# Second network's weight conversion moved off GpSimd, and the fourth and fifth chunk cut at 512 and 384 tokens

## Chip, cores and metric

The kernel runs on one core of a Trainium2 chip. The metric is the device time of one execution in microseconds (us). Engines are named as the profile names them: PE is TensorE, DVE is VectorE, ACT is ScalarE, POOL is GpSimd, SP is the engine whose queue issues the DMAs.

## What is computed

Attention over 4 batches, 8 heads, 576 positions and 64 channels gives 2304 tokens of 512 channels. They go through a gated feed-forward of width 1536 and then through a second feed-forward that takes the largest of three products, of width 768:

```python
scores = q @ k.T / 8                      # 4 heads: the last 32 positions; 4 heads: every 32nd position
x = softmax(where(mask, scores, -1e9)) @ v
g = x @ w_gate
x = (g * sigmoid(g) * (x @ w_val)) @ w_out
h = maximum(maximum(x @ w1, x @ w2), x @ w3)
out = h @ w2_out
```

The weights arrive as 64-bit numbers and are turned into 32-bit ones on the chip.

## The kernel before

**Tiles.** The 2304 tokens are 72 rows of 32 tokens (`ORDER`, l.43), cut into five chunks by `ROWS` (l.40): 512, 448, 448, 448 and 448 tokens. Each chunk goes through the first feed-forward in 12 blocks f of 128 hidden channels. A block is 36 matmuls: `emit_gate` (l.716) 12 into `ps_g`, `emit_val` (l.723) 12 into `ps_v`, `emit_out` (l.767) 12 into the four sums `ps_y`. Each product of 128 x 128 weights is three matmuls (l.701 to 703), since operands are split into a high and a low part. Between them lie a Silu on ACT (l.720), a multiply on DVE (l.727), a copy to the high part on ACT (l.733) and the low part on POOL (l.737). `ps_g` and `ps_v` share two PSUM buffers, so a product can start only when the one two before has been read.

**Order.** The first chunk (f = 0 to 11, with attention for the first two chunks and the conversion of the first network's weights) runs in an order written by hand, `FIRST`. The next four chunks are laid out by the loop at l.1080: block by block, with attention for the chunk after next to come spread over `attention_steps` (l.653), and with steps that convert the second network's weights. A scheduler then decides the order within each engine. `PACE` (l.35) says how many of those conversion steps each of the first ten blocks of a chunk brings; there are 60, five for each of 12 pairs of weight tiles.

**A conversion step.** For a pair (`pair_steps`, l.259): load two tiles of 512 KB; for each tile `size` and `rounding` on ACT (l.202, 205), `sign` (l.207), a clamp on DVE (l.219), `shift` and `rounded` on DVE (l.221, 229); then `combine` (l.263) makes the four sums of the seven-product scheme that the second network uses; then `part` (l.276) splits the results into high parts (ACT, l.281) and low parts (l.282) and stores them to DRAM in eight DMAs. `sign` has two forms: on ACT, for keys that stand in `ON_SCALAR` among the first network's tiles, or on POOL, for all others. With the first form `shift` has one input, with the second two.

**Strided attention.** Of four heads, the rows that PE doesn't take are done by `Unit` (l.567) on DVE: up to six rows at once, multiplies and reductions (l.600, 603, 622, 625), then transposes on PE (l.632).

**The seam.** After block f = 9 of the last chunk (`SEAM`) the attention buffers are freed, `load_y` (l.827) loads the first tokens of the second network, and `Factors.combine` and `Factors.split` (l.805, 812) make its operands during f = 10 and f = 11, in an order that is fixed by hand. The second network (l.858) then runs 1512 matmuls of 384 columns. All loads and stores are issued by SP, in order; the reloads of the first network's weights for each block (l.1018) stand in the same queue as the loads and stores of the conversion.

Of the kernel before, what the change touches and what calls it, by code (L numbers as in the profile page):

```python
# [7 lines left out]
F32 = mybir.dt.float32  # L8
# [5 lines left out]
ALU = mybir.AluOpType  # L14
AX = mybir.AxisListType

B, H, S, D = 4, 8, 576, 64
# [3 lines left out]
NI = S // STRIDE  # L21

LR = 2
# [8 lines left out]

PASSES = [1, 2, 0]

PACE = [0, 0.7, 1.4, 1.4, 3.1]

PACED = 10
NK = DM // 128

ROWS = [0, 16, 30, 44, 58, 72]  # L40


ORDER = [*range(16), *range(18, 72), 16, 17]
# [50 lines left out]
def tile_attention_swiglu_maxout(  # L94
# [13 lines left out]
    nc = tc.nc  # L108
# [31 lines left out]
    def f32(ap):  # L140
        return ap.bitcast(F32)
# [49 lines left out]
    made = {}  # L191

    def signed(key):
        return key in order and order.index(key) in ON_SCALAR

    def words(key):
        if key not in made:
# [61 lines left out]
    def pair_steps(i, g):  # L259
        keys = [(i, 2 * g), (i, 2 * g + 1)]  # L260
        made = {}

        def combine():
            w1t, w2t = (cvt.pop(k) for k in keys)
            s12 = wpool.tile([128, 512], F32, name="s12", tag="w")
            s4 = wpool.tile([128, 512], F32, name="s4", tag="w")[:, :256]
            a11, a12, a21, a22 = w1t[:, :256], w1t[:, 256:], w2t[:, :256], w2t[:, 256:]
            if i == 3:
                a12, a21 = a21, a12
            nc.vector.tensor_tensor(s12[:, :256], a21, a22, ALU.add)  # L270
            nc.vector.tensor_tensor(s12[:, 256:], s12[:, :256], a11, ALU.subtract)
            nc.gpsimd.tensor_tensor(a21, a11, a21, ALU.subtract)
            nc.vector.tensor_tensor(s4, a12, s12[:, 256:], ALU.subtract)
            made["full"] = [w1t, w2t, s12, s4]

        def part():
            dst = wsdr[i, g].rearrange("p (c s n) -> p c s n", c=7, s=2)
            for n, full in enumerate(made.pop("full")):
                w = full.shape[1]
                hi = wpool.tile([128, 512], F32R, name="whi", tag="w")[:, :w]  # L280
                nc.scalar.activation(hi, full, AF.Copy)
                (nc.gpsimd if n % 2 else nc.vector).tensor_tensor(full, full, f32(hi), ALU.subtract)
                for p, src in enumerate((f32(hi), full)):
                    nc.sync.dma_start(
                        dst[:, 2 * n:2 * n + w // 256, p], src.rearrange("p (c n) -> p c n", n=256)
                    )

        return [
            lambda: [load(k, w2[k[1], :, k[0], :]) for k in keys],
            lambda: convert(keys[0]),  # L290
            lambda: convert(keys[1]),
            combine,
            part,
        ]

# [228 lines left out]
    def local_block(g, home=None):  # L524


        def dst(src, us):
            for c, i0, i1, o in pieces(LR * g[0], LR * (g[-1] + 1)):
                t, w = slice(i0 * STRIDE, i1 * STRIDE), slice(o * STRIDE, (o + i1 - i0) * STRIDE)
                xh, xl = x_tile(c)  # L530
                yield xh[:, 0:2, t], xl[:, 0:2, t], src[:, :, w]

        return Block((locqk, locv), g[0], KB, [mask[0 if n % (NI // LR) == 0 else 1] for n in g], dst, home=home)
# [33 lines left out]
    class Unit:  # L567
# [36 lines left out]

        def softmax(self):
            sc, n, jn = self.sc, self.n, self.jn
            mx = tiny.tile([128, 6], F32, name="smx")[:, :n]
            nc.vector.tensor_reduce(mx, sc, AX.X, ALU.max)
            nc.vector.tensor_tensor(sc, sc, mx[:, :, None].to_broadcast([128, n, jn]), ALU.subtract)
            nc.scalar.activation(sc, sc, AF.Exp, scale=SCALE)  # L610
            sums = tiny.tile([128, 6], F32, name="ssum")[:, :n]
            nc.vector.tensor_reduce(sums, sc, AX.X, ALU.add)
            nc.vector.tensor_scalar(sums, sums, 1.0e-9, None, ALU.add)
            nc.vector.reciprocal(sums, sums)
            nc.vector.tensor_tensor(sc, sc, sums[:, :, None].to_broadcast([128, n, jn]), ALU.mult)
            self.o = st_p[0].tile([128, 6, D], F32, name="sto")

        def pv(self, r, eng):
            i = self.i0 + r
# [25 lines left out]

    def attention_blocks(c):
        rows = ORDER[ROWS[c]:ROWS[c + 1]]
        blocks = [local_block(g) for g in joined([r // LR for r in rows[::LR]])]
        if c == 1:
            blocks += [strided_block((st1qk, st1v), 1, g) for g in pairs(range(STRIDE // ON_PE[1][2]))]  # L650
        return blocks

    def attention_steps(c):

        steps = [[] for _ in range(15)]
        rows = ORDER[ROWS[c]:ROWS[c + 1]]
        eng = nc.vector
        blocks = attention_blocks(c)
        at = [0, 0, 4, 4, 8]
        for n, blk in enumerate(blocks):  # L660
            s0 = at[n]
            wait = 3 if c == 2 and s0 == 0 else 0
            steps[max(0, s0 - 2)].append(blk.load)
            if n % 2 and s0 == at[n - 1]:
                steps[s0].append(lambda a=blocks[n - 1], b=blk: a.scores_with(b))
                steps[s0 + wait].append(lambda a=blocks[n - 1], b=blk: (a.softmax(eng), b.softmax(eng)))
            elif n + 1 == len(blocks) or s0 != at[n + 1]:
                steps[s0].append(lambda blk=blk: (blk.scores(), blk.softmax(eng)))
            steps[s0 + (4 if wait else 1)].append(lambda blk=blk: blk.transpose(nc.scalar))
            if n % 2 and s0 == at[n - 1]:  # L670
                steps[s0 + (5 if wait else 2)].append(lambda a=blocks[n - 1], b=blk: (a.outputs_with(b), a.split(), b.split()))
            elif n + 1 == len(blocks) or s0 != at[n + 1]:
                steps[s0 + 2].append(blk.pv)
        units = []
        on_pe = {n: rows for n, rows, _ in ON_PE}
        left = [r for r in rows if r % NI >= on_pe.get(r // NI, 0)]
        while left:
            i = left[0]
            n = 1
            while n < len(left) and left[n] == i + n and (i + n) % NI % 6:  # L680
                n += 1
            units.append(Unit(i // NI, i % NI, n))
            left = left[n:]
        s0 = 0
        for u in units:
            steps[s0].append(u.load)
            steps[s0].append(u.begin)
            for r in range(u.n):
                steps[s0 + (2 * r // u.n)].append(lambda u=u, r=r: u.qk(r, eng))
            steps[s0 + 2].append(u.softmax)  # L690
            for r in range(u.n):
                steps[s0 + 2 + (2 * r // u.n)].append(lambda u=u, r=r: u.pv(r, eng))
            for r in range(0, u.n, 3):
                steps[s0 + 5 + r // 3].append(lambda u=u, r=r: u.out(r))
            s0 += 4
        return steps


# [555 lines left out]
```

## Time and profile before

| | us |
|---|---|
| median of 3 runs | 785.13 (785.03 to 786.27) |
| the profiled execution | 786.19 |
| its span, first to last instruction | 784.4 |
| PE busy | 767.7 (98%) |
| DVE busy | 613.2 (78%) |
| ACT busy | 400.9 (51%) |
| POOL busy | 230.8 (29%) |

The profile follows one execution. Busy times are sums over instructions of an engine; PE's matmuls overlap, so its busy time says little about how fast they follow each other, and the starts of successive rows in the timeline say it instead. The first chunk ends at about 143 us, the last chunk of the first network runs from 428 to 516 us, the second network from there to the end.

### The profile page before, as it was taken

The page shows a single profiled execution, that of the slowest core. Times are in us where ns is not written, and L with a number is a line of the kernel's source. Part 1 is how long each engine was busy: PE and PEld are TensorE (multiplying, and loading weights), DVE is VectorE, ACT ScalarE, POOL GpSimd, SP SyncE. Part 2 cuts the span into 40 slices and gives each one's busy share as a digit, 9 for nine tenths or more (in the row PEclk, how much of TensorE's full clock was granted, in tenths as well). Part 3 has the DMA queues.
Part 4 walks back from the last instruction along what each step waited for, and adds up shares of the span by engine and source line. Part 5 has one row for each costly group of instructions (what it writes and reads, how often), then busy time and mean ns, then how long its engine had stood idle before and what let it go on. Part 6 is the DMA issues. An engine that isn't in the chain of part 4 may idle for free.

```text
span 784.4 us, 13322 instructions
## 1 busy us (share of the span) xinstructions
PE 767.7 (98%) x4642; PEld 705.2 (90%) x4642; DVE 613.2 (78%) x1206; ACT 400.9 (51%) x925; POOL 230.8 (29%) x226
## 2 busy tenths in 40 slices
PE   5899999999999999999999999999999999999998
PEld 4677788888998998988899999999999999999998
DVE  5999999798959899799796777754689377855683
ACT  6999997644544636545342545432335233433342
POOL 2533332012221432325242556420124111321120
PEclk9999999999999999999999999999999999999999
DMA  9989886987657896847787999997675976878722
GB/s 274 369 277 320 306 351 236 372 252 230 221 188 222 285 293 222 267 168 256 255 286 267 314 378 392 342 377 274 242 276 199 414 270 264 276 280 355 276 101 81
DMA packets 75595, 216.26 MB, mean 276 GB/s; under 512 B 8488, under 2 KB 42024, under 8 KB 70920
## 3 DMA queue, kind: packets, MB, share of 16 engines
q1 hardware_dynamic: 75528, 215.41, 77.8%
q8 instruction: 37, 0.61, 0.3%
q14 instruction: 30, 0.25, 0.1%
HBM read 171.34 MB, written 44.04 MB: 275 GB/s over the span
## 4 chain that ended last, share of the span: by engine, by line
PE 85%; DVE 9%; ACT 3%; issue 1%; DMA 1%; POOL 1%; SPq 0%; DVEq 0%; ACTq 0%
PE ps_a L858 19%; PE ps_c L858 10%; PE ps_v L701 6%; PE ps_y L701 5%; PE ps_y L702 5%; PE ps_v L703 5%; PE ps_y L703 5%; PE ps_v L702 5%; PE ps_g L703 5%; PE ps_g L702 5%; PE ps_g L701 5%; PE ps_b L858 5%; DVE w L231 1%; PE ps_a L504 1%; PE ps_a L462 1%
## 5 line engine op out<-in xcount | busy, mean ns | idle before, releaser
L737 POOL TENSOR_TENSOR hl<-ht,hh 128x448 fp32r<-128x448 f32 x47 | 62.0, 1320 | 215.3 <-ACT hh L733 197.2
L869 ACT ACTIVATE s<-ps_a 128x384 f32<-128x384 f32 x99 | 48.5, 490 | 131.7 <-PE ps_a L858 131.7
L701 PE MATMUL ps_v<-xh,w_v 128*128 128x448 f32 (+1 forms) x240 | 90.8, 379 | 2.1 <-DVE ht L727 1.8
L701 PE MATMUL ps_g<-xh,wh_g 128*128 128x448 f32 (+1 forms) x240 | 89.9, 375 | 1.2 <-DVE ht L760 1.1
L702 PE MATMUL ps_y<-hl,w_o 128*128 128x448 f32 (+1 forms) x240 | 89.6, 373 | 0.0
L702 PE MATMUL ps_g<-xl,wh_g 128*128 128x448 f32 (+1 forms) x240 | 89.5, 373 | 0.0
L703 PE MATMUL ps_g<-xh,wl_g 128*128 128x448 f32 (+1 forms) x240 | 89.3, 372 | 0.0
L703 PE MATMUL ps_v<-xh,w_v 128*128 128x448 f32 (+1 forms) x240 | 89.2, 372 | 0.1
L703 PE MATMUL ps_y<-hh,w_o 128*128 128x448 f32 (+1 forms) x240 | 89.2, 372 | 0.0
L702 PE MATMUL ps_v<-xl,w_v 128*128 128x448 f32 (+1 forms) x240 | 88.9, 370 | 0.0
L733 ACT ACTIVATE hh<-ht 128x448 fp32r<-128x448 f32 (+1 forms) x60 | 35.3, 588 | 94.8 <-DVE ht L727 85.4
L701 PE MATMUL ps_y<-hh,w_o 128*128 128x448 f32 (+1 forms) x240 | 83.6, 376 | 0.0
L808 POOL TENSOR_TENSOR rT<-t,rT 128x384 f32<-128x384 f32 x9 | 12.5, 1392 | 147.1 <-DVE rT L807 147.1
L858 PE MATMUL ps_a<-y0hT,wr 128*128 128x384 f32 x162 | 54.1, 334 | 0.0
L858 PE MATMUL ps_a<-y1hT,wr 128*128 128x384 f32 x162 | 54.1, 334 | 0.0
L701 PEld LDWEIGHTS ps_v<-xh,w_v 128*128 128x128 f32 x240 | 45.1, 188 | 8.1 <-DVE ht L727 2.4
L701 PEld LDWEIGHTS ps_g<-xh,wh_g 128*128 128x128 f32 x240 | 45.1, 188 | 6.8 <-DVE ht L760 1.5
L703 PEld LDWEIGHTS ps_v<-xh,w_v 128*128 128x128 f32 x240 | 45.1, 188 | 5.5 <-DVE w_v L251 0.5
L701 PEld LDWEIGHTS ps_y<-hh,w_o 128*128 128x128 f32 x240 | 45.1, 188 | 5.2
L702 PEld LDWEIGHTS ps_g<-xl,wh_g 128*128 128x128 f32 x240 | 45.1, 188 | 5.1 <-DVE xl L522 0.3
L703 PEld LDWEIGHTS ps_g<-xh,wl_g 128*128 128x128 f32 x240 | 45.1, 188 | 5.1
L703 PEld LDWEIGHTS ps_y<-hh,w_o 128*128 128x128 f32 x240 | 45.1, 188 | 5.0 <-DVE w_o L251 0.3
(257 smaller groups left out, 2070.4 us busy)
## 6 DMA issues: line engine op xcount, KB each, us to landing
wr<-wsdr SPq DMA_DIRECT2D x36, 1792.0 KB, 8.1
raw<-in_w_dram SPq DMA_DIRECT2D x60, 512.0 KB, 6.3
w_v<-wvdr SPq DMA_DIRECT2D x48, 512.0 KB, 4.5
w_o<-wodr SPq DMA_DIRECT2D x48, 512.0 KB, 5.1
wsdr<-whi SPq DMA_DIRECT2D x36, 256.0 KB, 3.4
wvdr<-w_v SPq DMA_DIRECT2D x12, 512.0 KB, 4.6
wodr<-w_o SPq DMA_DIRECT2D x12, 512.0 KB, 6.6
wsdr<-w SPq DMA_DIRECT2D x24, 256.0 KB, 3.9
```

What stands on the lines that cost most here:

```text
L231: nc.vector.tensor_tensor(w, w, q, ALU.add)
L462: nc.tensor.transpose(ps[:sm.shape[2], g * 128:(g + 1) * 128], sm[:, g], ident)
L504: ins = nc.tensor.matmul(ps[j * D:(j + 1) * D, at:at + nq], v, p, start=True, stop=True).ins
L701: nc.tensor.matmul(ps, wh, xh, start=first, stop=False)
L702: nc.tensor.matmul(ps, wh, xl, start=False, stop=False)
L703: nc.tensor.matmul(ps, wl, xh, start=False, stop=last)
L733: return nc.scalar.activation(hs[c, f][0], t, AF.Copy).ins
L737: return eng.tensor_tensor(hl, t, f32(hh), ALU.subtract).ins
L808: nc.gpsimd.tensor_tensor(b12, self.raw["B22"], b12, ALU.subtract)
L858: nc.tensor.matmul(ps, w[:, c, a, ks], b, start=first and n == q == 0, stop=last and n == len(wts) - 1 and q == 2, skip_group_check=True,)
L869: nc.scalar.activation(s, ps, AF.Copy)
```

## The change

It does four things. The fourth and fifth chunk get 16 and 12 rows, 512 and 384 tokens, where they had 14 each. Tiles of the second network take the ACT form of `sign` and the one-input form of `shift`, and their difference in `combine` and all their low parts go to DVE. `PACE` is 0.8, 1.3, 2.0 and 2.0 steps per block in the second to fifth chunk, where it was 0.7, 1.4, 1.4 and 3.1. A `Unit` takes up to eight rows and is cut evenly within a batch, where it was cut at multiples of six; the steps of a chunk's units are spread over 12 divided by their number.

```diff
-PACE = [0, 0.7, 1.4, 1.4, 3.1]
+PACE = [0, 0.8, 1.3, 2.0, 2.0]
+UNIT = 8
-ROWS = [0, 16, 30, 44, 58, 72]
+ROWS = [0, 16, 30, 44, 60, 72]
     def signed(key):
-        return key in order and order.index(key) in ON_SCALAR
+        return key not in order or order.index(key) in ON_SCALAR
...
-            nc.gpsimd.tensor_tensor(a21, a11, a21, ALU.subtract)
+            nc.vector.tensor_tensor(a21, a11, a21, ALU.subtract)
...
-                (nc.gpsimd if n % 2 else nc.vector).tensor_tensor(full, full, f32(hi), ALU.subtract)
+                nc.vector.tensor_tensor(full, full, f32(hi), ALU.subtract)
...
-            while n < len(left) and left[n] == i + n and (i + n) % NI % 6:
+            while n < len(left) and left[n] == i + n and (i + n) % NI:
                 n += 1
-            units.append(Unit(i // NI, i % NI, n))
+            parts = -(-n // UNIT)
+            for p in range(parts):
+                a, b = n * p // parts, n * (p + 1) // parts
+                units.append(Unit(i // NI, i % NI + a, b - a))
             left = left[n:]
-        s0 = 0
-        for u in units:
+        span = 12 // len(units)
+        for u, s0 in zip(units, range(0, 12, span)):
+            half = span // 2
             steps[s0].append(u.load)
             steps[s0].append(u.begin)
             for r in range(u.n):
-                steps[s0 + (2 * r // u.n)].append(lambda u=u, r=r: u.qk(r, eng))
-            steps[s0 + 2].append(u.softmax)
+                steps[s0 + half * r // u.n].append(lambda u=u, r=r: u.qk(r, eng))
+            steps[s0 + half].append(u.softmax)
             for r in range(u.n):
-                steps[s0 + 2 + (2 * r // u.n)].append(lambda u=u, r=r: u.pv(r, eng))
+                steps[s0 + half + half * r // u.n].append(lambda u=u, r=r: u.pv(r, eng))
             for r in range(0, u.n, 3):
-                steps[s0 + 5 + r // 3].append(lambda u=u, r=r: u.out(r))
-            s0 += 4
+                steps[min(14, s0 + span + 1 + r // 3)].append(lambda u=u, r=r: u.out(r))
```

Lines up to about 200 have moved down by two in the changed kernel, those behind `attention_steps` by six, so l.202 is l.204 there, l.720 is l.726 and l.733 is l.739.

The first place is ACT's queue at the start of the fourth chunk, between the Silu of its second block and that of its third (`ht<-ps_g`). Before:

```order
L720 ACTIVATE ht<-ps_g 128x448
L733 ACTIVATE hh<-ht 128x448
L202 ACTIVATE w_4124<-raw 128x512
L205 ACTIVATE q<-raw 128x512
L783 ACTIVATE ysb<-ps_y 128x448 x2
L440 ACT_TABLE_LOAD
L440 ACTIVATE sm,stat<-sm,stat 128x96 x6
L720 ACT_TABLE_LOAD
L720 ACTIVATE ht<-ps_g 128x448
```

With the change:

```order
L726 ACTIVATE ht<-ps_g 128x512
L739 ACTIVATE hh<-ht 128x512
L204 ACTIVATE w_4137<-raw 128x512
L207 ACTIVATE q<-raw 128x512
L204 ACTIVATE w_4145<-raw 128x512
L207 ACTIVATE q<-raw 128x512
L789 ACTIVATE ysb<-ps_y 128x448 x2
L213 ACTIVATE q<-raw,mh 128x512 x2
L442 ACT_TABLE_LOAD
L442 ACTIVATE sm,stat<-sm,stat 128x96 x4
L726 ACT_TABLE_LOAD
L726 ACTIVATE ht<-ps_g 128x512
```

One more tile's size and rounding and the two signs (l.213) stand there now, and four exponentials in place of six.

The second place is DVE's queue at the seam: the multiplies (`ht<-ht,ps_v`), from that of f = 9 to that of f = 10 before, where the last pair's two low parts (l.282) stand ahead of f = 9:

```order
L282 TENSOR_TENSOR w_5596<-w_5596,whi 128x512
L282 TENSOR_TENSOR s_5611<-s_5611,whi 128x512
L727 SCALAR_TENSOR_TENSOR ht<-ht,ps_v 128x448
L807 TENSOR_TENSOR rT_5785<-rT_5762,y0lB_5759 128x384
L178 TENSOR_TENSOR y0lB_5759<-y0lB_5759,y0hB_5792 128x384
L809 TENSOR_TENSOR rT_5788<-y0lB_5765,rT_5785 128x384
L178 TENSOR_TENSOR y0lT_5803<-rT_5785,y0hT_5802 128x384
L178 TENSOR_TENSOR y0lT_5799<-rT_5788,y0hT_5798 128x384
L810 TENSOR_TENSOR rT_5790<-y0lB_5768,rT_5788 128x384
L178 TENSOR_TENSOR y0lB_5768<-y0lB_5768,y0hB_5795 128x384
L727 SCALAR_TENSOR_TENSOR ht<-ht,ps_v 128x448
```

With the change, from the combination that now stands ahead of the multiply of f = 9:

```order
L813 TENSOR_TENSOR rT_5776<-rT_5753,y0lB_5750 128x384
L733 SCALAR_TENSOR_TENSOR ht<-ht,ps_v 128x384
L180 TENSOR_TENSOR y0lB_5750<-y0lB_5750,y0hB_5783 128x384
L815 TENSOR_TENSOR rT_5779<-y0lB_5756,rT_5776 128x384
L180 TENSOR_TENSOR y0lT_5794<-rT_5776,y0hT_5793 128x384
L816 TENSOR_TENSOR rT_5781<-y0lB_5759,rT_5779 128x384
L284 TENSOR_TENSOR w_5587<-w_5587,whi 128x512
L284 TENSOR_TENSOR w_5644<-w_5644,whi 128x512
L284 TENSOR_TENSOR s_5651<-s_5651,whi 128x512
L284 TENSOR_TENSOR s_5652<-s_5652,whi 128x256
L180 TENSOR_TENSOR y0lB_5759<-y0lB_5759,y0hB_5786 128x384
L180 TENSOR_TENSOR y0lT_5790<-rT_5779,y0hT_5789 128x384
```

The four low parts of the last pair (l.284), all on DVE, stand behind the multiply of f = 9 now, and the first combination of y (l.813) ahead of it; the multiply of f = 10 follows the last row shown.

## Rows read from the trace of the kernel before

**Rows 1.** The page, part 1: busy us (share of the span), instructions.

```profile
PE 767.7 (98%) x4642; PEld 705.2 (90%) x4642; DVE 613.2 (78%) x1206; ACT 400.9 (51%) x925; POOL 230.8 (29%) x226
```

**Rows 2.** PE's waits from 143 us on: us in total, times, longest.

```profile
PE ps_v L701 <- DVE ht L727: 1.8, 2, 1.4
PE ps_v L701 <- ACT ht L720: 0.3, 1, 0.3
```

**Rows 3.** Busy times by stretch; columns as in the first line.

```profile
core 0: us, PE busy (x) PEld busy (x) DVE busy (x) ACT busy (x) POOL busy (x), PEclk, DMA share, GB/s
...
238.00:331.00 93.00, 91.56 (x553) 82.93 (x552) 84.69 (x176) 49.97 (x112) 29.23 (x27) 1.00 0.80 263
...
428.20:516.00 87.80, 87.80 (x436) 81.37 (x435) 64.54 (x86) 40.66 (x81) 45.75 (x42) 1.00 1.00 362
```

**Rows 4.** PE's timeline, three stretches: start us, us, instruction.

```profile
47.81 0.50 PE L701 MATMUL ps_v<-xh,w_v 128*128 128x512 f32 x1
48.15 0.39 PE L702 MATMUL ps_v<-xl,w_v 128*128 128x512 f32 x1
...
50.67 0.39 PE L701 MATMUL ps_y<-hh,w_o 128*128 128x512 f32 x1
...
113.19 0.39 PE L701 MATMUL ps_g<-xh,wh_g 128*128 128x512 f32 x1
...
115.91 0.39 PE L701 MATMUL ps_y<-hh,w_o 128*128 128x512 f32 x1
...
450.36 0.36 PE L701 MATMUL ps_g<-xh,wh_g 128*128 128x448 f32 x1
...
457.66 0.36 PE L701 MATMUL ps_g<-xh,wh_g 128*128 128x448 f32 x1
```

**Rows 5.** The chain that ended last, second network: start us, us, what.

```profile
519.78 1.04 PE ps_b L858 x6
```

**Rows 6.** DVE's groups by line and shape: busy us, mean ns, idle before.

```profile
L227 DVE SCALAR_TENSOR_TENSOR w<-w,raw 128x512 int32<-128x512 int32 x39 | 30.5, 791 | 3.3 <-POOL raw L213 2.6 <-POOL w L219 0.5
L219 DVE TENSOR_SCALAR w<-w 128x512 f32<-128x512 f32 x24 | 18.2, 761 | 7.7 <-ACT w L202 7.5
L282 DVE TENSOR_TENSOR w<-w,whi 128x512 f32<-128x512 f32 x12 | 14.6, 1218 | 6.1 <-ACT whi L281 5.5 <-ACT ht L720 0.6
L273 DVE TENSOR_TENSOR s<-w,s 128x256 f32<-128x256 f32 x12 | 10.1, 844 | 0.2
L270 DVE TENSOR_TENSOR s<-w 128x256 f32<-128x256 f32 x9 | 3.7, 413 | 0.1
L600 DVE TENSOR_TENSOR pr<-stk,stq 128x512 f32<-128x512 f32 x2 | 1.4, 688 | 0.0
```

**Rows 7.** DVE's timeline, a clamp in the third chunk.

```profile
305.40 0.43 DVE L219 TENSOR_SCALAR w<-w 128x512 f32<-128x512 f32 x1
```

**Rows 8.** ACT's groups by line and shape: the signs of the first network.

```profile
L211 ACT ACTIVATE q<-raw,mh 128x512 f16<-128x512 int32 x21 | 18.3, 876 | 0.0
```

**Rows 9.** ACT's timeline at the start of the fourth chunk: two Silus.

```profile
345.75 0.55 ACT L720 ACTIVATE ht<-ps_g 128x448 f32<-128x448 f32 x1 [2.00 <-PE ps_g L703]
...
353.66 0.55 ACT L720 ACTIVATE ht<-ps_g 128x448 f32<-128x448 f32 x1
```

**Rows 10.** DVE's timeline at the seam; in brackets the idle time before and its releaser.

```profile
499.81 0.55 DVE L807 TENSOR_TENSOR rT<-rT,y0lB 128x384 f32<-128x384 f32 x1
...
509.38 1.36 DVE L807 TENSOR_TENSOR rT<-rT,y1lB 128x384 f32<-128x384 f32 x1
...
513.89 0.62 DVE L727 SCALAR_TENSOR_TENSOR ht<-ht,ps_v 128x448 f32<-128x448 f32 x1 [0.33 <-PE ps_v L703]
```

**Rows 11.** POOL's groups by line and shape: a combination of the second network's operands.

```profile
L808 POOL TENSOR_TENSOR rT<-y1lB,rT 128x384 f32<-128x384 f32 x3 | 4.2, 1390 | 4.3 <-DVE rT L807 4.3
```

**Rows 12.** DMA issues: count, KB each, median us to landing.

```profile
wr<-wsdr SPq DMA_DIRECT2D x36, 1792.0 KB, 8.1
raw<-in_w_dram SPq DMA_DIRECT2D x60, 512.0 KB, 6.3
...
y0lB<-ydr SPq DMA_DIRECT2D x5, 192.0 KB, 5.6
```

More of the change, by code (lines that the diff above doesn't have):

```diff
@@ L606, in softmax @@
             sc, n, jn = self.sc, self.n, self.jn
-            mx = tiny.tile([128, 6], F32, name="smx")[:, :n]
+            mx = tiny.tile([128, UNIT], F32, name="smx")[:, :n]
             nc.vector.tensor_reduce(mx, sc, AX.X, ALU.max)
@@ L610, in softmax @@
             nc.scalar.activation(sc, sc, AF.Exp, scale=SCALE)
-            sums = tiny.tile([128, 6], F32, name="ssum")[:, :n]
+            sums = tiny.tile([128, UNIT], F32, name="ssum")[:, :n]
             nc.vector.tensor_reduce(sums, sc, AX.X, ALU.add)
@@ L615, in softmax @@
             nc.vector.tensor_tensor(sc, sc, sums[:, :, None].to_broadcast([128, n, jn]), ALU.mult)
-            self.o = st_p[0].tile([128, 6, D], F32, name="sto")
+            self.o = st_p[0].tile([128, UNIT, D], F32, name="sto")
         def pv(self, r, eng):
@@ L647, in attention_blocks @@
         rows = ORDER[ROWS[c]:ROWS[c + 1]]
-        blocks = [local_block(g) for g in joined([r // LR for r in rows[::LR]])]
+        before = {r // LR for r in ORDER[:ROWS[c]]}
+        blocks = [local_block(g) for g in joined([g for g in dict.fromkeys(r // LR for r in rows) if g not in before])]
         if c == 1:
```

## Prediction

> **What bounds the kernel now.** I read three views, from the whole to the place. The page's first part: TensorE (PE) is busy 98% of a 784.4 us span [rows 1]. The list of PE's waits from 143 us on, where the first chunk ends and with it the order written out by hand, has three waits: two for VectorE (DVE), 1.8 us in all, the longest 1.44, and one of 0.3 us for ScalarE (ACT) [rows 2]. The busy times by stage: PE is full and at the full clock, 2.4 GHz, in each; DVE is the next to be full, 84.7 of 93.0 us in the third chunk; in the last chunk it has 64.5 of 87.8, but there the DMA engines' share reads 1.00 at 362 GB/s [rows 3]. So a change pays in two ways only: by what a matmul costs, or by a moment at which PE waits. The first chunk and the second feed-forward (from 516 us) keep their order, so only the four later chunks and the seam into the second network can move.
>
> **1. Widths.** The fourth and the fifth chunk have 432 matmuls each (12 blocks of 36), before and after. At 448 tokens 36 follow each other in 7.30 us, 202.8 ns each; at 512 the pace is 226.7 ns in a quiet stretch (12 in 2.72 us) and 229.1 soon after a break (11 in 2.52 us) [rows 4]; at 384 it is 173.3 (6 in 1.04 us) [rows 5]. Less the columns at 2.4 GHz (213.3, 186.7 and 160.0 ns), 512 and 384 pay 13.4 and 13.3 ns, and 448 pays 16.1. The fourth chunk still has attention's small products inside, so I take 228.5 ns there, and for both chunks of before 203.1, a little over the quiet row: 432 x (228.5 + 173.3 - 2 x 203.1) = **-1.9 us**. Ends: -2.4 by the quiet rows; 0 if the extra 2.8 ns belong to this stage and not to the width, for no row shows 384 in it. Then the breaks: small products split the stream 40 times after the first chunk in the built order, 43 times before, and a break costs 0.11 us (47.81 to 48.15 instead of 0.23) [rows 4]: **-0.3 us**.
>
> **2. Conversions off GpSimd (POOL).** POOL loses 60 operations, five for each of 12 pairs of weight tiles: two signs, two low parts, one difference. DVE gains 36 of them: 12 low parts of 512, 12 of 256, 12 differences of 256. Beside POOL's share of the same work, DVE's own low parts of 512 took 1218 ns and its difference of 256 took 844; such operations apart from it took 688 (512) and 413 (256) [rows 6]. So the new ones cost 12 x 0.69 + 24 x 0.41 = 18.1 us. The old ones should shed 24 x 0.53 (the row of 12 shown has a twin) + 12 x 0.43 = 17.9, and the 24 clamps, at 761 [rows 6] against 430 where one ran alone [rows 7], 24 x 0.33 = 7.9. The shift turns from a form with two inputs, 791 [rows 6], into one with one input, which I price like the clamp: 24 x 0.36 = 8.6. DVE ends 16 us lighter, not heavier.
>
> The rule that speaks against this is in the Trainium skill (Perfetto Trace Analysis, Optimizing Scalar/DVE Operations): offloading from a saturated DVE, even to GpSimd, may make sense. The same section warns that the two share a read port, and rows 6 side with the warning. By the offloading rule alone DVE would be 18.1 us heavier, and this part would be rival (e).
>
> What is it worth? PE was kept for 1.44 us and for 0.36 us by a VectorE multiply that stood behind conversions and attention in DVE's queue [rows 2]. With DVE 16 us lighter I take **-1.8 us**, all of it; the other end is 0 (new waits take their place: attention's rows of the fourth chunk come as two units of eight now and crowd the second and third chunk).
>
> **3. Signs on ACT.** A sign takes 876 ns on ACT [rows 8]; 24 are 21 us on an engine that is half idle, except at one place. At the start of the fourth chunk ACT goes from one Silu to the next, through conversions, evictions, a table load, six exponentials and another table load, from 345.75 to 353.66 [rows 9], and PE is 0.3 us late for that second Silu [rows 2]. In the built order there is one more size and rounding on this way (1.1 us), there are two signs (1.75) and two exponentials less (-0.7): +2.1 us. PE's 36 matmuls meanwhile last 36 x 25.7 ns = 0.9 us longer. **+1.3 us**; ends 0 (if a lighter DVE lets the way begin sooner) and +2.1.
>
> **4. Pace and the seam.** In the last chunk the steps per block fall from 3.1 to 2.0, and the last pair is done one block later, between the multiplies of f = 9 and f = 10. From the multiply of f = 9 to that of f = 11 DVE now has 12 splits and combinations of 384 (0.55 each where alone, as at 499.81 [rows 10]), four low parts (2.4) and two multiplies (1.1): 10.1 us. POOL's five operations in that time, some 1.3 us each (1.39 for a combination [rows 11]), I charge at half their length, 3.3. And a combination now stands ahead of the multiply of f = 9 and waits for a load of y, 5.6 us [rows 12], which leaves SP's queue when the products of f = 7 end; the multiply is due 24 matmuls, 4.2 us, later, so with the combination it is up to 2.0 us late. Together 15.4 us. Against that stand two blocks of PE, 12.5, and 2.0 of slack (PE needs the split result 3.6 us after the product of f = 11 ends, and the way over DVE, ACT and DVE takes 1.6). **+0.9 us**; ends 0, and 7.3 if every one of the 12 is held up as long as the one at 509.38 was, 1.36 [rows 10], which is 9.7 us in place of the 3.3. Before, the multiply of f = 11 waited for PE, not PE for it [rows 10]. The fourth chunk's higher pace (1.4 to 2.0) is hidden by blocks that are 0.9 us longer; without that cover it would be rival (e). In the last chunk 19 steps instead of 25 ease the DMAs: nothing is gained by that while PE does not wait for a weight.
>
> **Sum:** -1.9 - 0.3 - 1.8 + 1.3 + 0.9 = -1.8 us. The profiled execution took 786.19 us, 784.4 of span and 1.8 around it, so it becomes 784.4. It stands 1.06 above the median of 785.13; the forecast is **783.3 us**. A measurement of this kernel can tell about 0.2% from no change, 1.57 us: below 783.56 is faster, above 786.70 slower.
>
> **Rivals.**
> (a) *Everything hides* (0.21): quiet pace, no ACT miss, no seam: -2.4 - 0.3 - 1.8 = -4.5 us against the median, 780.6 us. For it: DVE is 16 us lighter. Against: ACT's way is longer by any reading.
> (b) *The widths even out* (0.14): the extra 2.8 ns go with the stage, the first term is 0: 785.2 us. For it: 512 runs at 229 after breaks. Against: quiet 448 and quiet 512 are rows of one stage. The Trainium skill (TensorE: Matmul & The Clock Gate, Back-to-back issue gap) gives an isolated gap of N/2.4 ns and a constant, by which 512 and 384 cost what two of 448 cost: this rival. Rows 4 and 5 have one constant at 512 and 384 and a larger one at 448.
> (c) *The seam* (0.11), the one that ends slower: DVE's queue holds a combination that waits for y, then the last pair's low parts, then more splits, and the multiplies that PE needs stand behind each. At the upper end, 7.3 instead of 0.9: 789.7 us. It decides from a stall of 4.3 us on. For it: a combination beside POOL took 1.36 us [rows 10]. Against: POOL has lost the low parts it had there.
> (d) *DMA sets the last chunk* (0.07): 87.8 us at 362 GB/s are 31.8 MB [rows 3]. Six steps fewer, of five to a pair of 2.9 MB (two loads of 0.5 and stores of the 1.8 that a later load reads back [rows 12]), take 3.5 off; 28.3 MB at that rate need 78.2 us where PE needs 12 x 6.24 = 74.9: +3.3, 786.6 us. Against: PE did not wait at a share of 1.00.
> (e) *DVE gets no relief* (0.05), the part that doesn't do what it says: the moved operations run at contended prices and the old waits stay: +1.8, 785.1 us.
>
> **Numbers.** The forecast has the rest, 0.42; its own range is 781.8 to 784.8, and some 0.27 of it lies below 783.56. Faster: 0.27 + 0.21 = 0.48. Slower: 0.09 of (c), 0.03 of (d). Same: 0.40. The range 780.5 to 787.0 reaches (a), (b), (d) and (e) and leaves out most of (c) and the tails.
>
> **What would show it.** Right: 512 near 228 ns and 384 near 173 in PE's timeline; low parts near 0.69 us on DVE; no PE wait for VectorE of 1 us in the third chunk; one of 1 to 2 us for ACT early in the fourth; PE waiting under 2 us between the last block and the second network. Wrong: 384 at 176 or more (b); a seam wait over 4 us (c); waits for weight reloads in the last chunk (d).

## The result and the profile after

The changed kernel takes **790.96 us** (median of 6, 789.41 to 792.22) where the kernel before takes 785.08: ratio 1.007, 95% interval 1.0057 to 1.0084, some 5.5 us (5.9 between the two medians). The forecast was 783.3 us, faster; it is slower, outside the range. The profiled execution took 792.22 us with a span of 790.0. In three of the six executions, the profiled one among them, the mean granted clock is 0.993; these took 791.5 to 792.2 us, the others 789.4 to 790.5. In the profiled one the granted clock is 0.84 from 15 to 25 us and 0.88 from 25 to 40, in the first chunk. There the instructions of every engine stand in the same order in both kernels, and the kernel before has executions with a mean clock of 0.996 and 0.993 too, so I do not count what such a stretch adds, up to 2 us, as an effect of the change; why three of these six show 0.993 is not shown.

The page, part 1, as in [rows 1]:

```profile
PE 770.7 (98%) x4642; PEld 703.1 (89%) x4642; DVE 601.8 (76%) x1238; ACT 419.6 (53%) x950; POOL 169.1 (21%) x165
```

Against [rows 1] DVE is 11.4 us lighter, POOL 61.7; ACT has 18.7 more. The engine that was to be relieved was relieved, and the kernel is slower. PE's waits from 143 us on, as in [rows 2] (us in total, times, longest):

```profile
PE ps_v L707 <- DVE ht L733: 2.5, 2, 2.2
PE ps_v L707 <- ACT ht L726: 1.8, 1, 1.8
PE ps_b L864 <- DVE ysb L787: 0.9, 1, 0.9
PE ps_y L707 <- ACT hh L739: 0.6, 1, 0.6
PE ps_g L707 <- ACT ht L726: 0.3, 1, 0.3
```

2.1 us of waits have become 6.1, of which 5.5 stand in three places: the start of the third chunk (2.2), the start of the fourth (1.8), the seam (0.9 and 0.6).

**The third chunk's start**, in its third block. PE's timeline at the first of these waits:

```profile
257.47 0.36 PE L709 MATMUL ps_g<-xh,wl_g 128*128 128x448 f32 x1
260.01 0.47 PE L707 MATMUL ps_v<-xh,w_v 128*128 128x448 f32 x1 [2.18 <-DVE ht L733]
...
261.08 0.57 PE L708 MATMUL ps_v<-xl,w_v 128*128 128x448 f32 x1
261.46 0.57 PE L709 MATMUL ps_v<-xh,w_v 128*128 128x448 f32 x1
```

Behind the wait matmuls of 448 start 0.38 us apart in place of 0.20. The window of these microseconds shows the granted clock at 0.54, that is mostly at 1.2 GHz, in the column after the busy times:

```profile
260.40:264.00 3.60, 3.60 (x12) 3.23 (x11) 3.60 (x7) 2.00 (x3) 1.14 (x1) 0.54 0.53 156
```

Counted from start to start, less the quiet pace of 0.203, the wait cost 2.3 us and the slow stretch 1.6. What DVE did meanwhile is seen in the row products of the attention units (tile `pr`) from one multiply to the next, in the windows of DVE (each begins some 0.24 us ahead of its multiply). Columns: window, us, busy (x), clock, DMA share, GB/s.

```profile
232.92:239.11 6.19, 3.03 (x3) 1.00 0.66 199
239.11:249.03 9.92, 8.06 (x8) 1.00 0.82 248
249.03:259.11 10.08, 7.31 (x7) 1.00 0.67 219
```

The same three blocks of the kernel before:

```profile
227.26:234.97 7.71, 0.00 (x0) 1.00 0.61 204
234.97:247.85 12.88, 11.52 (x11) 1.00 0.54 167
247.85:254.56 6.71, 3.58 (x3) 1.00 0.99 313
```

Before, DVE had no row product in the first of these blocks, then 11.5 us, then a light block in which it caught up. After, two heavy blocks follow each other, 20.0 us for two, and the second multiply comes too late. The two blocks alone do not tell the kernels apart, for before they last 12.88 and 6.71 us, 19.6 together. What differs as well is how DVE came into them. Before, it had nothing left to do ahead of its multiply of 235.20 and waited for PE:

```profile
235.20 0.62 DVE L727 SCALAR_TENSOR_TENSOR ht<-ht,ps_v 128x448 f32<-128x448 f32 x1 [7.09 <-PE ps_a L632]
```

Over six blocks, up to the multiply behind the two heavy ones, DVE (the third busy time of a row) stood idle for 9.6 us before and for 2.4 us after. The first row is of the kernel before, the second of the changed one:

```profile
206.02:254.80 48.78, 48.78 (x319) 44.18 (x318) 39.18 (x84) 23.48 (x63) 10.99 (x12) 1.00 0.69 220
205.07:259.35 54.28, 52.44 (x343) 46.99 (x342) 51.87 (x103) 27.51 (x72) 9.54 (x7) 1.00 0.66 205
```

The reason lies in the loop that lays the attention out: a chunk's attention is spread from three blocks before the chunk ahead of it begins to the end of that chunk (it is the next chunk's, not that of the chunk after next). Under the old cut only two of the fourth chunk's rows had their first products in the last three blocks of the second chunk; the next six began in the third chunk. A unit of eight puts the first products of all eight there, and their second products into the third chunk's first blocks.

Over the whole stage (238 to 331 us) DVE is even less busy than in [rows 3], 80.9 us against 84.7:

```profile
238.00:331.00 93.00, 90.82 (x556) 81.70 (x555) 80.90 (x185) 54.33 (x120) 17.28 (x14) 0.98 0.75 244
```

**The fourth chunk's start.** ACT's timeline, the two Silus of [rows 9] with the signs between, and PE behind them:

```profile
352.05 0.60 ACT L726 ACTIVATE ht<-ps_g 128x512 f32<-128x512 f32 x1 [1.50 <-PE ps_g L709]
...
356.17 1.60 ACT L213 ACTIVATE q<-raw,mh 128x512 f16<-128x512 int32 x2
...
361.94 0.60 ACT L726 ACTIVATE ht<-ps_g 128x512 f32<-128x512 f32 x1
```

```profile
362.59 0.50 PE L707 MATMUL ps_v<-xh,w_v 128*128 128x512 f32 x1 [1.77 <-ACT ht L726]
```

The way from Silu to Silu is 9.89 us, 1.98 longer than before.

**The seam.** DVE's timeline, where [rows 10] stood:

```profile
506.29 0.56 DVE L813 TENSOR_TENSOR rT<-rT,y0lB 128x384 f32<-128x384 f32 x1 [1.25 <-DMA y0lB<-ydr]
...
513.63 0.54 DVE L733 SCALAR_TENSOR_TENSOR ht<-ht,ps_v 128x384 f32<-128x384 f32 x1
515.59 0.65 DVE L180 TENSOR_TENSOR y0lT<-rT,y0hT 128x384 fp32r<-128x384 f32 x1 [1.42 <-ACT y0hT L177]
...
519.40 0.56 DVE L816 TENSOR_TENSOR rT<-y1lB,rT 128x384 f32<-128x384 f32 x1 [1.28 <-DMA y1lB<-ydr]
...
520.81 0.55 DVE L733 SCALAR_TENSOR_TENSOR ht<-ht,ps_v 128x384 f32<-128x384 f32 x1
```

DVE stands idle for ACT and for a load (1.42 and 1.28 us) with the last multiply queued behind. PE's gaps there are 2.1 us in all.

**The widths** came as forecast: quiet blocks of 36 matmuls at 512 and at 384 in PE's timeline take 8.16 and 6.24 us, 226.7 and 173.3 ns each.

```profile
419.79 0.39 PE L707 MATMUL ps_g<-xh,wh_g 128*128 128x512 f32 x1
...
427.95 0.39 PE L707 MATMUL ps_g<-xh,wh_g 128*128 128x512 f32 x1
...
457.72 0.33 PE L707 MATMUL ps_g<-xh,wh_g 128*128 128x384 f32 x1
...
463.96 0.33 PE L707 MATMUL ps_g<-xh,wh_g 128*128 128x384 f32 x1
```

From the second chunk to the end, summed over PE's intervals in the two profiles (us, after less before): widths -2.2, the old waits -1.7, the third chunk's start +2.3 and +1.6, the fourth's +1.6, the seam +2.1, small products and the rest +0.5: +4.2 us. The other 1.6 of the two profiled executions' difference is there before the second chunk's first gate product.

### The profile page after: what moved, and what is told of

It is laid out like the page before. It is cut to its first block, busy times and chain, and to the rows that moved or that the text cites. A ratio compares the mean times of both kernels' runs of the same rounds, so it can differ in the third digit from the quotient of the medians.

```text
span 790.0 us, 13239 instructions
## 1 busy us (share of the span) xinstructions
PE 770.7 (98%) x4642; PEld 703.1 (89%) x4642; DVE 601.8 (76%) x1238; ACT 419.6 (53%) x950; POOL 169.1 (21%) x165
## 4 chain that ended last, share of the span: by engine, by line
PE 80%; DVE 11%; ACT 4%; DMA 3%; issue 2%; SPq 1%; DVEq 0%; ACTq 0%
PE ps_a L864 19%; PE ps_c L864 9%; PE ps_v L707 5%; PE ps_y L707 5%; PE ps_v L709 5%; PE ps_v L708 5%; PE ps_y L708 5%; PE ps_y L709 5%; PE ps_b L864 5%; PE ps_g L707 5%; PE ps_g L708 5%; PE ps_g L709 5%; DVE pr L624 2%; DVE w L233 1%; PE ps_a L506 1%
## 5 line engine op out<-in xcount | busy, mean ns | idle before, releaser
L743 POOL TENSOR_TENSOR hl<-ht,hh 128x448 fp32r<-128x448 f32 (+2 forms) x47 | 62.3, 1327 | 279.7 <-ACT hh L739 266.3
L707 PE MATMUL ps_v<-xh,w_v 128*128 128x512 f32 (+2 forms) x240 | 91.0, 379 | 4.3 <-DVE ht L733 2.5
L707 PE MATMUL ps_g<-xh,wh_g 128*128 128x512 f32 (+2 forms) x240 | 90.3, 376 | 0.3 <-ACT ht L726 0.3
L708 PE MATMUL ps_g<-xl,wh_g 128*128 128x512 f32 (+2 forms) x240 | 89.8, 374 | 0.4 <-DVE xl L524 0.4
L708 PE MATMUL ps_v<-xl,w_v 128*128 128x512 f32 (+2 forms) x240 | 89.3, 372 | 0.0
L709 PE MATMUL ps_v<-xh,w_v 128*128 128x512 f32 (+2 forms) x240 | 89.3, 372 | 0.0
L709 PE MATMUL ps_g<-xh,wl_g 128*128 128x512 f32 (+2 forms) x240 | 89.2, 371 | 0.0
L708 PE MATMUL ps_y<-hl,w_o 128*128 128x512 f32 (+2 forms) x240 | 89.1, 371 | 0.0
L709 PE MATMUL ps_y<-hh,w_o 128*128 128x512 f32 (+2 forms) x240 | 88.9, 370 | 0.0
L707 PE MATMUL ps_y<-hh,w_o 128*128 128x512 f32 (+2 forms) x240 | 86.3, 376 | 0.6 <-ACT hh L739 0.6
L739 ACT ACTIVATE hh<-ht 128x512 fp32r<-128x512 f32 (+2 forms) x60 | 35.3, 589 | 80.1 <-DVE ht L733 69.3
L733 DVE SCALAR_TENSOR_TENSOR ht<-ht,ps_v 128x448 f32<-128x448 f32 (+2 forms) x48 | 29.6, 616 | 43.8 <-PE ps_v L709 42.3
```

Source lines behind the costliest of these rows:

```text
L707: nc.tensor.matmul(ps, wh, xh, start=first, stop=False)
L708: nc.tensor.matmul(ps, wh, xl, start=False, stop=False)
L709: nc.tensor.matmul(ps, wl, xh, start=False, stop=last)
L733: m = nc.vector.scalar_tensor_tensor(t, t, 1.0, ps[:, :n], ALU.mult, ALU.mult).ins
L739: return nc.scalar.activation(hs[c, f][0], t, AF.Copy).ins
L743: return eng.tensor_tensor(hl, t, f32(hh), ALU.subtract).ins
```

## The experiments

Every ratio is to the kernel before, run on the same chip. Each expectation names a theory by a letter (U, units; A, signs on ACT; P, pace) and a rival. "Gap" is time between two starts on PE over the quiet pace; the three places are the third chunk's start, the fourth's, and the seam.

| run | median us | ratio, 95% interval | gaps at the three places, us |
|---|---|---|---|
| conversion alone | 786.57 | 1.0014 (1.0002 to 1.0026) | none; 1.2; none |
| rows, pace, units alone | 789.69 | 1.0056 (1.0040 to 1.0071) | 3.0; 0.4; 2.5 |
| change, old rows | 791.44 | 1.0080 (1.0062 to 1.0098) | 1.9; 3.1 + 1.6 half clock; 0.5 |
| change, units of 4 | 789.27 | 1.0052 (1.0032 to 1.0071) | 0.6; 1.7; 2.5 |
| change, old pace | 791.14 | 1.0069 (1.0050 to 1.0089) | 1.4; under 0.3; 4.7 + 1.6 half clock |
| change, signs on POOL | 789.79 | 1.0045 (1.0030 to 1.0061) | 3.0 + 1.7 half clock; 0.5; 1.7 |
| units alone | 790.84 | 1.0062 (1.0045 to 1.0079) | 4.1, a block or two earlier; 0.4; 1.0 |
| change, units over 8 and 4 steps | 789.98 | 1.0055 (1.0035 to 1.0075) | 2.1 + 1.6 half clock; 2.5; 1.0 |
| change, cut 2 + 6 | 788.63 | 1.0040 (1.0027 to 1.0053) | 1.5; 1.7; 1.4 |
| cut 2 + 6, signs on POOL | 786.66 | 1.0023 (1.0010 to 1.0036) | 1.5; 1.6; 1.7 |
| the same, pace 2.4 | 785.00 | 0.9998 (0.9986 to 1.0010) | 1.9; 1.6; 0.4 |
| low parts alone | 785.42 | 1.0000 (0.9988 to 1.0012) | none; 0.4; none |
| old cut, rows, low parts, pace 2.4 | 784.85 | 0.9995 (0.9983 to 1.0007) | 0.4; 0.4; 0.4 |
| old cut, rows, pace 2.4 alone | 785.38 | 1.0000 (0.9990 to 1.0010) | 0.4; 0.4; 0.6 |
| old cut, rows, whole conversion, pace 2.4 | 786.70 | 1.0020 (1.0007 to 1.0033) | 1.6; 1.6; 0.4 |
| change, pace 2.4 | 788.79 | 1.0046 (1.0031 to 1.0062) | 2.1 + 1.7 half clock; 1.9; 0.4 |

**Conversion alone**: the kernel before with the three lines of the conversion from the change's diff (`signed`, `a21`, the low parts).

> The kernel before with the conversion move alone (signs on ACT, difference and low parts on DVE); rows, pace and units as before. Theory U (the units of eight rows crowd VectorE at the start of the third chunk, TensorE waits 2.2 us there and then runs at half clock for 3.4 us; the move itself is good): 783 to 785 us, VectorE about 11 us lighter, no wait of 1 us for VectorE's multiply in the third chunk, at most one wait of 1 to 2 us for ACT at the start of the fourth. Rival C (the move is what costs: longer queues on ACT and DVE): 788 to 791 us, with the 2 us wait at the start of the third chunk present although the units are the old ones.

Neither theory's range: 0.14% slower, 1.6 us above U's. No wait of the third chunk is left but 0.3 us, but one of 1.1 us for ACT has come in the fourth. DVE is at 600.0 us, 13 lighter. What it gains it gives back.

**Rows, pace and units alone**: the change without these three lines.

> The changed kernel with the old conversion (signs, difference and half of the low parts on POOL); the new rows, pace and units stay. Theory U: 789 to 793 us, the wait at the start of the third chunk stays at 2 us or more, because the units stay and DVE is heavier. Rival C: 783 to 786 us, no wait over 1 us there.

U's side: +0.56%, with a gap of 3.0 us at the third chunk's start, so rival C falls. But the late instruction is now a Silu on ACT. It stands behind a table load, eight exponentials and another table load, 9.4 us after the Silu before it, and only 0.85 and 0.27 us of that way are waits for DVE. This run shows the place and size of the loss, not that DVE's queue alone makes it. The fourth chunk's gap is 0.4: the signs are back on POOL.

**The change with old rows.**

```diff
-ROWS = [0, 16, 30, 44, 60, 72]
+ROWS = [0, 16, 30, 44, 58, 72]
```

> The changed kernel with 448 and 448 tokens in the fourth and fifth chunk instead of 512 and 384. The fourth chunk's attention still has one unit of eight rows (and one of six). Theory U: the wait at the start of the third chunk stays (1 to 2.2 us), and the widths give back 1.9 us: 791 to 793 us. Rival W (the 512 tokens with their two units of eight and the longer blocks are what costs): 785 to 788 us.

791.4 as U has it, with a gap of 1.9 us at the third chunk's start: 512 tokens are not needed for the loss. The half-clock stretch is at the fourth chunk's start here.

**Units of four.**

```diff
-UNIT = 8
+UNIT = 4
```

> The changed kernel with units of at most four rows, spread over three steps each; all else stays. Theory U: the wait at the start of the third chunk falls under 0.5 us and no half-clock stretch follows it; about 4 us come back: 786 to 788 us. Rival (the wait is set by conversions and the local attention in VectorE's queue, not by the units' size): the wait stays over 1.5 us, 789.5 to 792 us.

Half of each: the wait at the third chunk's start fell to 0.6, but 1.0 to 1.7 us of gaps stand at three places of the fourth chunk instead.

**The change with the old pace.**

```diff
-PACE = [0, 0.8, 1.3, 2.0, 2.0]
+PACE = [0, 0.7, 1.4, 1.4, 3.1]
```

> The changed kernel with the old pace of the conversion steps (0.7, 1.4, 1.4, 3.1 per block). Theory P (the pace, which puts the last pair's low parts behind the multiply of the tenth block, makes the seam, where TensorE loses 2.1 us in gaps): the gaps at the seam fall under 0.7 us, and 788.5 to 789.7 us in all. Rival N (the seam is short because blocks of 384 tokens give VectorE 6.24 us a block instead of 7.30): the gaps stay at 1.5 to 2.5 us, and 790 to 792 us.

P's forecast fell, and the 4.7 us of gaps are above the rival's too. The seam became worse, in its list of waits by the reloads of the first network's weights, for which PE waits in no other run:

```profile
PE ps_y L707 <- DMA w_o<-wodr: 1.7, 1, 1.7
PE ps_v L707 <- DMA w_v<-wvdr: 1.3, 2, 0.9
```

With 25 steps in the short blocks of 384 tokens PE waits for these reloads, with the change's 19 it does not.

**The change with the signs on POOL.**

```diff
-        return key not in order or order.index(key) in ON_SCALAR
+        return key in order and order.index(key) in ON_SCALAR
```

> The changed kernel with the signs of the second network on POOL again (and the two-input shift); difference and low parts stay on VectorE. Theory A (the signs on ACT make TensorE wait 1.9 us at the start of the fourth chunk): that gap falls under 0.6 us, 1.3 us or more come back, 788.5 to 789.7 us; the wait at the start of the third chunk stays at 2 us. Rival (the wait for ACT comes from elsewhere, the shift in POOL's presence costs VectorE more): the gap stays over 1.2 us, or VectorE's waits grow by as much, 790.5 to 792 us.

Theory A holds: the gap goes from 1.9 to 0.5 us, the ratio from 1.0070 to 1.0045. The wait at the third chunk's start is longer than in the change, 2.8 us against 2.2, and is for a Silu on ACT, as in the run without the conversion.

**Units alone**: the change with rows, pace and conversion as before.

> The kernel before with the new units alone (up to eight rows, cut evenly, steps spread over 12); rows, pace and conversion as before. Theory U (the units' cut and spread make the wait at the start of the third chunk): a wait of 1.5 to 3 us there, 787 to 790 us. Rival (it takes the new pace or the conversion on VectorE as well): no wait over 0.8 us there, 784 to 786 us.

+0.62%: the new units alone make almost as large a loss, 0.8 us above U's range. But U's place is missed: the gaps, of 0.8, 1.5 and 1.8 us, stand from 220 to 235 us, before the third chunk begins, and at its start no wait is over 0.3 us, as the rival had it. There the first products of the unit of eight meet the last rows of the chunk ahead. So the units are enough for a loss of this size; where it falls depends on the other edits too.

**Other steps for the same units.**

```diff
-        span = 12 // len(units)
-        for u, s0 in zip(units, range(0, 12, span)):
+        spans = [8, 4] if c == 3 else [12 // len(units)] * len(units)
+        for n, (u, span) in enumerate(zip(units, spans)):
+            s0 = sum(spans[:n])
```

> The changed kernel with one edit: the fourth chunk's first unit, whose eight rows are 704 to 1152 wide, gets 8 of the 12 steps and the second, whose rows are 64 to 512 wide, the other 4. Theory U: VectorE's row products between two multiplies fall from 9.1 and 7.3 us to under 7 around the start of the third chunk, the wait there falls under 0.6 us, no half-clock stretch follows it, and 786.5 to 788 us come out. Rival (the wait is made by the local attention and the evictions that stand there, or it comes back later in the chunk): a wait of over 1.5 us somewhere in the third chunk, 789.5 to 791.5 us.

The wait stayed, with the rival's numbers, and the reason is in DVE's windows for `pr` of this run, which at the two blocks are those of the change to 0.02 us:

```profile
237.17:247.08 9.91, 8.04 (x8) 1.00 0.76 253
247.08:257.17 10.09, 7.33 (x7) 1.00 0.67 218
```

The scheduler put the same products between the same multiplies, whatever their step; the edit did not do what it was to do, so it says nothing against U and nothing for it.

**The wide rows cut in two and six.**

```diff
+            cuts = [n * p // parts for p in range(parts + 1)]
+            if c == 3 and i % NI == 10:
+                cuts = [0, 2, n]
```

> The changed kernel with one edit: the eight wide rows of the fourth chunk's attention (704 to 1152 wide) are cut into a unit of two and one of six, as the old cut would have them; the eight narrow rows stay one unit. VectorE's queue around the start of the third chunk then holds no longer all eight rows' second products within two blocks. Theory U: TensorE's wait of 2.3 us there and the half-clock stretch behind it (1.6 us) go, the rest of the loss (fourth chunk's start, seam) stays: 786.5 to 788 us, ratio to the kernel before 1.002 to 1.004. Rival (whatever the units, this layout leaves a wait of 2 us somewhere in the third chunk): ratio 1.005 to 1.008.

U holds in place and in the ratio, 1.0040 against 1.0070, with no half-clock stretch. (With three units in place of two each has 4 steps, not 6: cut and spread of the units change together here, as they do in the change.) DVE's windows for `pr` are those of before again, but small gaps for the copy of `ps_y` and for the low part on POOL (1.5 us) have come:

```profile
229.19:237.36 8.17, 0.00 (x0) 1.00 0.37 128
237.36:250.29 12.93, 11.44 (x11) 1.00 0.51 160
250.29:255.41 5.12, 3.58 (x3) 1.00 1.03 313
```

**The same with signs on POOL, and then with pace 2.4.**

> The run above with the signs of the second network on POOL again as well. Theory U with theory A (the signs on ACT cost 1.5 us at the start of the fourth chunk): the two losses add, only the seam's 2 us and the widths' gain of 2.2 us are left, and the wait of the old kernel in the third chunk is gone: 784 to 786 us, ratio 0.998 to 1.001. Rival (the losses do not add, one wait takes the place of the other): ratio 1.002 to 1.005.

1.0023, in the rival's range, and by the rival's mechanism: the gap at the fourth chunk's start is 1.6 still, now for DVE, where row products of the fifth chunk's two units of five stand. One wait has taken the place of another.

```diff
-PACE = [0, 0.8, 1.3, 2.0, 2.0]
+PACE = [0, 0.8, 1.3, 2.0, 2.4]
```

> The run above with 2.4 steps per block in the last chunk instead of 2.0, so that the last pair is done a block earlier. If the last pair's low parts make the seam's waits: the gaps there fall from 2 us to under 1, ratio 0.996 to 0.999. If 384 tokens do (6.24 us a block): the gaps stay at 1.5 to 2.5 us, or DMA waits of 1 us come in the last blocks, ratio as in the run above or 0.001 more.

The last pair does make the seam: gaps from 1.7 to 0.4 us, and no DMA wait. The ratio is a little above the range. Three edits have taken the ratio from 1.0070 by 1.0040 and 1.0023 to 0.9998.

**Low parts and difference alone**, in the kernel before.

> The kernel before with the difference and the low parts on VectorE alone; signs on POOL, rows, pace and units as before. Theory (the part of the conversion move that relieves VectorE is good by the 1.7 us wait in the third chunk, and only the signs on ACT give it back): 783 to 784.5 us, ratio 0.997 to 0.999, gap under 0.6 us at the start of the fourth chunk. Rival (the old wait goes but another takes its place): ratio 0.9995 to 1.002.

The rival: no change. The old wait in the third chunk is 0.9 us in place of 1.4, not gone. DVE is busy for 612.9 us, as before.

**The old cut with the new rows**, in three runs: with the low parts on DVE, with no conversion moved, and with the whole of it. The cut, in the changed kernel, in place of the loop over `parts`:

```diff
-            while n < len(left) and left[n] == i + n and (i + n) % NI:
+            while n < len(left) and left[n] == i + n and ((i + n) % NI % 6 or c == 3 and (i + n) % NI == 6):
```

> New rows (512 and 384 tokens), units cut at multiples of six as before, but for the eight narrow rows of the fourth chunk, which stay one unit; 2.4 steps per block in the last chunk; difference and low parts on VectorE, signs on POOL. Theory U: with the old cut no wait of 1 us for VectorE is left at the start of the third and the fourth chunk, the widths' 2.2 us and the old wait's 1.7 come through less 0.4 at the seam: 781.5 to 784 us, ratio 0.995 to 0.998, faster than both kernels. Rival G (what the widths give, the longer attention queue of 16 rows in one chunk takes back in waits): ratio 0.999 to 1.002.

> The run above with the whole conversion as before: rows, the least cut that they need, and pace alone. If the widths pay by themselves: 783 to 784.5 us, ratio 0.997 to 0.999, TensorE's quiet blocks of 8.16 and 6.24 us and not more waits than before. Rival G: ratio 1.000 to 1.003, with new waits of 2 us in sum in the third and fourth chunk.

> The run before the last (difference and low parts on VectorE) with the signs on ACT too. Theory A: a wait of 1.2 to 2 us for ACT at the start of the fourth chunk that the run without it does not have, ratio 0.0015 to 0.0025 above it. Rival (the wait depends on the cut, not on the signs): no more than 0.0005 above it.

The crowding is gone, but so is the gain: 0.9995 and 1.0000, the rival G's ratios both times. With the widths alone PE's matmuls are 2.4 us shorter in the profile and the waits and breaks as much longer. G's new waits of 2 us are not among them: PE's listed waits are 2.8 us in sum where they were 2.1, the longest of them (1.1) the old one late in the third chunk, and the rest is spread in pieces of under 0.5 us. With the signs on ACT too, 0.0025 come on top, and the wait for ACT at the fourth chunk's start is back (1.4 us), as theory A has it; one of 1.2 us for ACT has come in the third chunk beside it.

**The change with pace 2.4 alone.**

> The changed kernel with 2.4 steps per block in the last chunk and nothing else changed. If the seam is a loss by itself: gaps there fall from 2.1 us to 0.4, 788.5 to 789.5 us, ratio 1.0045 to 1.0057, the other waits unchanged. Rival (the losses are not independent): ratio 1.006 to 1.0085.

1.0046: the seam by itself, about 0.0024. The list of PE's waits is that of the change without its two rows of the seam:

```profile
PE ps_v L707 <- DVE ht L733: 2.3, 2, 1.9
PE ps_v L707 <- ACT ht L726: 1.8, 1, 1.8
PE ps_g L707 <- ACT ht L726: 0.3, 1, 0.3
```

**Together.** Undone one at a time in the changed kernel, pace, cut and signs give back 0.0024, 0.0030 and 0.0025; together 0.0072. The sum of the three, 0.0079, is the joint effect within intervals of some 0.002 for such a difference: about 1.9, 2.4 and 2.0 us. Place by place they do not simply add: with the cut undone, undoing the signs gave 0.0017, and another wait stood where theirs had been. What is left of the change is worth nothing that can be measured. No version beats the kernel before: the best, at 0.9995, has 1 in its interval.

## Why the prediction was wrong, step by step

**Bound.** Right: what counted was what a matmul costs and the moments at which PE waits, and these are three places that the trace names. That a matmul can cost more behind a wait, at the lower clock, was not seen.

**1. Widths, -1.9.** Right in the profile (-2.2 in matmuls here, -2.4 with the widths alone; 384 at 173.3 ns, so rival (b) fell as a statement on matmuls). By the formula for an isolated gap in the Trainium skill (TensorE: Matmul & The Clock Gate, Back-to-back issue gap) there would have been no gain here; rows of 226.7, 202.8 and 173.3 ns say otherwise. But the term as a gain in time was not borne out: rows, the least cut and a pace for them alone measured 1.0000. The -0.3 for fewer breaks cannot be seen apart: small products and the rest came out at +0.5.

**2. Conversions off POOL, -1.8: the step that failed.** DVE became 11.4 us lighter, not 16; these are its groups in the profile after, for [rows 6]:

```profile
L284 DVE TENSOR_TENSOR w<-w,whi 128x512 f32<-128x512 f32 x24 | 18.3, 794 | 5.1 <-ACT whi L283 5.0
L284 DVE TENSOR_TENSOR s<-s,whi 128x512 f32<-128x512 f32 x12 | 8.2, 680 | 0.0
L221 DVE TENSOR_SCALAR w<-w 128x512 f32<-128x512 f32 x24 | 14.8, 622 | 8.2 <-ACT w L204 6.9 <-DMA wsdr<-w 1.1
L274 DVE TENSOR_TENSOR w<-w,w 128x256 f32<-128x256 f32 x9 | 5.8, 645 | 0.0
```

The low parts fell from 1218 to 794 and 680 ns. The clamp (622) and the difference (645) took more than the 430 and 413 that I had. Two runs take the relief apart. With the low parts and the difference alone, 36 operations more on DVE and 36 fewer on POOL, DVE is busy for 612.9 us where it was for 613.2: the moved work came at no price, as the sum had it (18.1 against 17.9), and gave no relief. With the signs on ACT too, in the kernel before, it is 600.0; half of these 12.9 us are the shift's, whose two groups fell from 39.8 to 33.5 us with the one-input form. The warning in the Trainium skill (Perfetto Trace Analysis, Optimizing Scalar/DVE Operations) that moving work between these two engines might not help agrees with these runs: POOL's 36 operations were no relief to DVE while POOL had them. The 1.4 us wait did go in the changed kernel. What failed is the other end: "new waits take their place: attention's rows of the fourth chunk come as two units of eight now and crowd the second and third chunk" was written down and bounded at 0, as if new waits could at most cancel the old one. That edit, the units' cut, had no term of its own. It cost 2.3 us of wait and 1.6 of half clock in the profile, undoing it gave 2.4 us in time, and alone in the kernel before it made 0.62%. DVE's total over a stage was the wrong number: what counted was the row products between two multiplies in a row, and whether DVE came to them idle or behind. How much of it is the cut and how much the spread of the units over the steps is not shown.

**3. Signs, +1.3.** Right in place and size: the way grew by 1.98 us where +2.1 stood, a sign took 880 ns, PE's gap grew by 1.5. Undoing it gave 1.3 to 2.0 us in time.

**4. Pace and seam, +0.9.** Right mechanism, too small: 2.1 us of gaps, 1.9 in time. The idle waits of DVE for ACT's splits and for the second load of y (2.7 us together) were not in the sum; POOL's part was. Rival (c) needed 4.3 us and did not come, nor (d): in the change PE waited for no weight reload. With the old pace PE did wait for reloads, which is (d)'s sign.

**Sum.** With the losses as measured, 1.9 + 2.4 + 2.0 us over a remainder of nothing, 785.1 becomes 791.4; measured 790.96. The range failed because its upper end took in no loss from the one edit without a price. That a wait of 2 us can be followed by a stretch at 1.2 GHz was not in it either.

**Open.** Why the run with the old cut and low parts shows 1.8 us less on PE from the second chunk on in its profile and 0.9995 in time: single executions differ by some 2 us at their start. Which of the small waits eats the widths' gain was not taken apart.

## What to carry to other kernels

Price every edit of a change, also the one that only makes room for another: here the new cut of the attention rows, which had no price, cost 2.4 of some 6.3 us. Where an engine feeds a full one through a queue in order, add up what its queue holds between two instructions that are waited for, block by block, and carry over what the blocks ahead left undone; its total over a stage, and even its becoming lighter, says nothing on that. A bound of "nothing" for an effect whose mechanism is already written down has to be argued, not assumed.

## What the hardware showed that was not expected

The granted clock falls to half behind some waits, and the wait's length does not tell which. Two runs have the same wait of 2.80 us at the same place (PE's timeline; the first is rows, pace and units alone, the second the change with signs on POOL):

```profile
259.52 0.47 PE L707 MATMUL ps_v<-xh,w_v 128*128 128x448 f32 x1 [2.80 <-ACT ht L726]
259.83 0.36 PE L708 MATMUL ps_v<-xl,w_v 128*128 128x448 f32 x1
260.03 0.36 PE L709 MATMUL ps_v<-xh,w_v 128*128 128x448 f32 x1
```

```profile
258.84 0.52 PE L707 MATMUL ps_v<-xh,w_v 128*128 128x448 f32 x1 [2.80 <-ACT ht L726]
259.16 0.57 PE L708 MATMUL ps_v<-xl,w_v 128*128 128x448 f32 x1
259.53 0.57 PE L709 MATMUL ps_v<-xh,w_v 128*128 128x448 f32 x1
```

In the first the matmuls go on 0.20 us apart, in the second 0.37, and 1.7 us are lost on top of the wait. It is a matter of the kernel more than of the execution: the mean clock is 0.998 or less in all 6 executions of the second, in 1 of 5 of the first, and in all 6 of the changed kernel. It is not wholly so: the change with pace 2.4 has it behind a wait of 1.9 us in its profile, and one of its 6 executions has a mean clock of 1.000. What decides it is not shown here.
